# Splitting the load of the second K into three transfers

## The chip, the cores and the metric

The kernel runs on one core of a Trainium2 chip. The metric is device time in microseconds (us), the median of several runs. A core has a matrix engine (TensorE, PE in the profile, with its weight loads as PEld), a vector engine (VectorE, DVE), a scalar engine (ScalarE, ACT), GpSimd (POOL) and SyncE (SP), which here only issues transfers. Data are moved between the chip's main memory (HBM) and the on-chip memory (SBUF, 128 partitions) by sixteen DMA engines.

## The reference

It is the forward and backward pass of attention for one query row and 32 heads, with 8,192 keys and values of 128 numbers each, in bfloat16:

```python
scores = jnp.einsum('bhqd,bhkd->bhqk', q, k) * scale      # (1, 32, 1, 8192)
attn = softmax(scores, axis=-1)
out = jnp.einsum('bhqk,bhkd->bhqd', attn, v)
# and the gradients of out, for a given grad_out, to q, k and v
```

The outputs are `out`, dq, dk and dv. K and V are 64 MiB each and are read once; dk and dv are as large and are written once. dk is the outer product of ds (the gradient of the scores) and q, dv that of the attention weights p and grad_out.

## The kernel before

Heads are taken two at a time: sixteen pairs, `t` from 0 to 15. The K of a pair is one tile of 128 partitions by 128 rows by 128 numbers, 32 KiB a partition and 4 MiB in all; partition p holds 128 neighbouring rows, so that a whole load reads 32 KiB in one run for each partition (`rows_of`). The same holds for V. There are three buffers for K and two for V, used in turn (`Kt`, `Vt`).

For each pair K is turned by VectorE (`k_block`, L197) and multiplied with q on TensorE (L205), which gives the scores; softmax follows (`s_back` to `p_of`). V is turned by TensorE (`v_bank`, L269) and copied by ScalarE (L275), or turned by VectorE (`v_block`, L293), and multiplied with grad_out into dp (`v_scores`, `v_wide`). From p and dp comes ds. V and K are then contracted with p and ds (`contract`, L341) for out and dq. At last VectorE writes dv and dk over V and K in place (`outer`, L363), and from there they are stored (`store`, L373).

A buffer's round is therefore load, read, overwritten, stored, loaded again. In the loop over `t`, the load of K for `t + 2` (L540) waits for the store of dk of pair `t - 1` out of the same buffer, and the load of V for `t + 2` (L542) for the store of dv of pair `t`. Loads and stores of K and V are all issued by SP, in the program's order, on one queue: a transfer that waits holds up those behind it. The order of the work is written out by hand (`tc.manual_schedule`). Completion of transfers is told by eight semaphores used in turn; a ninth transfer is issued when the one eight places earlier has landed.

The change lies at the start, ahead of all this: q and grad_out, then V and K of pair 0 in four quarters each (8 KiB a partition), then K and V of pair 1 whole:

```python
    load_v(0, 4)
    load_k(0, 4)
    load_k(1)
    load_v(1)
```

The third K (`load_k(2)`, L410) is issued once pair 0 no longer uses that buffer as room for its turned V. K of pair 1 is first read by `k_block(1, 0)` inside the loop's first round, V of pair 1 by `v_part(1, 0)` near the end of that round.

Of the kernel before, what the change touches and what calls it, by code (L numbers as in the profile page):

```python
# [20 lines left out]
SL = 8  # L21
# [6 lines left out]
def kernel(  # L28
# [11 lines left out]
    nc = tc.nc  # L40
    P = 128
    _, H, S, D = k.shape
    HP = H // 2
    NT = 2 * S // P
# [27 lines left out]
    Kt = {t: k_in[t % K_BUFS] for t in range(HP)}  # L72
    Vt = {t: v_in[t % V_BUFS] for t in range(HP)}

    def rows_of(x, t, a, b):
        return x[0, 2 * t:2 * t + 2].rearrange("h s d -> (h s) d").rearrange("(p n) d -> p n d", p=P)[:, a:b, :]

    def load(x, X, t, parts):
        L = NT // parts
        for c in range(parts):  # L80
            nc.sync.dma_start(X[t][:, c * L:(c + 1) * L, :], rows_of(x, t, c * L, (c + 1) * L))

    def load_k(t, parts=1):
        load(k, Kt, t, parts)

    def load_v(t, parts=1):
        load(v, Vt, t, parts)
# [3 lines left out]
    nc.scalar.dma_start(rows[:, 1, :], grad_out.rearrange("b h s d -> (b h s) d"))  # L91
    load_v(0, 4)
    load_k(0, 4)
    load_k(1)
    load_v(1)

    ident = consts.tile([P, P], BF16)
# [477 lines left out]
```

## Time and profile before

| | |
|---|---|
| median of 3 runs | 635.55 us (635.55 to 635.78) |
| profiled execution | 635.36 us, its span 633.6 us |
| DMA queue q1 (all loads and stores of SP) | 268.47 MB, 99.2% of sixteen engines' time |
| VectorE busy | 558.9 us, 88% of the span |
| TensorE busy | 428.7 us, 68% |
| ScalarE busy | 158.0 us, 25% |
| a whole load of K or V, from issue to landing | 19.3 us, median |

The span runs from the first to the last instruction that the profiler recorded; some 1.8 us of the execution's time lie around it. The DMA share is the mean over the sixteen engines: 1.00 means that all of them moved data all the time, and 0.25 that four did. A transfer is spread over the engines, each of which sets a completion mark of its own when its part has landed; a wait for the transfer ends with the last mark. The trace has the time of each mark, but not the number of the engine that set it.

### The profile page before, as it was taken

How to read it: one execution, taken by the hardware profiler on the slowest of the kernel's cores; microseconds unless marked ns; L12 is line 12 of the kernel's file. 1: busy time of each engine (PE TensorE's matmuls, PEld its weight loads, DVE VectorE, ACT ScalarE, POOL GpSimd, SP SyncE). 2: the span in 40 equal slices, each digit the busy share in tenths (PEclk: the TensorE clock that was granted, in tenths of full speed). 3: DMA queues.
4: the chain of work that ended last, by engine and by line, in shares of the span. 5: the costliest groups of instructions: out<-in, count | busy, mean ns of one | idle time of the engine just before them, and what ended most of it. 6: DMA issues, size and time to landing. Idle time of an engine off the chain costs nothing.

```text
span 633.6 us, 7259 instructions
## 1 busy us (share of the span) xinstructions
PE 428.7 (68%) x2876; PEld 231.2 (36%) x2876; DVE 558.9 (88%) x662; ACT 158.0 (25%) x407; POOL 9.5 (1%) x27
## 2 busy tenths in 40 slices
PE   6767777766685765847766676765768658576860
PEld 5225335242341523315342332523425233152630
DVE  3788997999979899998998989899898899989793
ACT  6013416031230412204031130311303113040520
POOL 2000000000000000000000000000000000000000
PEclk9879888879789777798878798687986878887865
DMA  8999999999999999999999999999999999999997
GB/s 355 440 428 398 438 418 415 425 430 409 432 433 431 435 431 431 435 432 431 429 431 430 432 431 430 430 432 438 436 426 434 431 434 427 432 430 429 426 414 325
DMA packets 12177, 268.92 MB, mean 424 GB/s; under 512 B 1520, under 2 KB 1520, under 8 KB 1520
## 3 DMA queue, kind: packets, MB, share of 16 engines
q1 hardware_dynamic: 12096, 268.47, 99.2%
q8 instruction: 22, 0.36, 0.2%
q14 instruction: 11, 0.09, 0.0%
q10 hardware_dynamic: 48, 0.01, 0.0%
HBM read 134.23 MB, written 134.23 MB: 424 GB/s over the span
## 4 chain that ended last, share of the span: by engine, by line
DVE 38%; DMA 27%; PE 22%; issue 9%; ACT 2%; DVEq 0%; SPq 0%; ACTq 0%
DVE XK_sb L197 15%; DMA K<-in_k_dram 14%; DMA out_dram<-K 13%; DVE K L363 11%; PE T_ps L269 10%; DVE V L363 6%; PE dp_ps L303 5%; PE acc_p L341 3%; PE dp_ps L286 2%; ACT XV_sb L275 1%; DVE sT L212 1%; DVE dpT L312 1%; PE m_ps L220 1%; DMA V<-in_v_dram 1%; DVE ds_rep L331 1%
## 5 line engine op out<-in xcount | busy, mean ns | idle before, releaser
L205 PE MATMUL s_ps<-XK_sb,q_win 128*128 128x512 bf16 x512 | 148.6, 431 | 50.5 <-DVE XK_sb L197 48.3
L197 DVE STREAM_TRANSPOSE XK_sb<-K 128x1024 f32<-128x1024 f32 x128 | 152.2, 1221 | 3.5 <-DMA K<-in_k_dram 3.3
L363 DVE TENSOR_TENSOR V<-p_rep,qd 128x2048 bf16<-128x2048 bf16 x128 | 152.0, 1203 | 3.2 <-DMA K<-in_k_dram 2.0
L363 DVE TENSOR_TENSOR K<-ds_rep,qd 128x2048 bf16<-128x2048 bf16 x128 | 147.8, 1207 | 0.1
L269 PE MATMUL T_ps<-ident_f,V 128*128 128x128 f32 x640 | 108.1, 333 | 0.3 <-DMA V<-in_v_dram 0.2
L205 PEld LDWEIGHTS <-q_win 128*128 128x128 bf16 x512 | 53.4, 106 | 138.6 <-issue 102.7
L269 PEld LDWEIGHTS T_ps<-ident_f,V 128*128 128x128 f32 x640 | 97.5, 176 | 14.5 <-ACT XV_sb L275 1.6
L275 ACT COPY XV_sb<-T_ps 128x512 f32<-128x512 f32 x144 | 79.0, 586 | 78.7 <-PE T_ps L269 78.3
L293 DVE STREAM_TRANSPOSE XV_blk<-V 128x1024 f32<-128x1024 f32 x48 | 59.6, 1241 | 9.1 <-PE dp_ps L303 8.7
L341 PE MATMUL acc_ds<-K,win_ds 128*32 128x512 bf16 x512 | 47.8, 540 | 27.8 <-ACT win_ds L241 27.8
L220 PE MATMUL m_ps<-ident_f,top 128*128 128x128 f32 x16 | 6.2, 389 | 72.6 <-DVE top L219 72.6
L303 PE MATMUL dp_ps<-XV_blk,do_wide 128*128 128x512 bf16 x192 | 51.2, 399 | 0.0
L182 ACT COPY q_win<-q_blk 128x16 bf16<-128x16 bf16 x16 | 4.2, 260 | 156.7 <-PE s_ps L205 156.2
L341 PE MATMUL acc_p<-V,win_p 128*32 128x512 bf16 x512 | 32.1, 394 | 2.6 <-ACT win_p L241 2.4
L341 PEld LDWEIGHTS <-win_ds 128*32 128x32 bf16 x512 | 15.9, 122 | 48.1 <-ACT win_ds L241 27.2
L220 PEld LDWEIGHTS m_ps<-ident_f,top 128*128 128x128 f32 x16 | 2.6, 161 | 79.4 <-issue 71.4
L286 PE MATMUL dp_ps<-XV_sb,do_win 128*32 128x512 bf16 x288 | 24.3, 413 | 8.1 <-ACT XV_sb L275 8.1
L230 ACT ACTIVATE e<-sT,nbias 128x128 f32<-128x128 f32 x16 | 8.2, 515 | 80.8 <-DVE nbias L227 80.8
L303 PEld LDWEIGHTS <-do_wide 128*128 128x128 bf16 x192 | 17.3, 100 | 28.3 <-issue 14.3
L312 DVE STREAM_TRANSPOSE dpT<-dp_ps 128x512 f32<-128x512 f32 x16 | 11.5, 717 | 13.9 <-PE dp_ps L303 13.0
L341 PEld LDWEIGHTS <-win_p 128*32 128x32 bf16 x512 | 13.0, 99 | 16.3 <-issue 6.7
L321 PE MATMUL m_ps<-pd,same 128*128 128x1 f32 x32 | 6.1, 260 | 18.8 <-DVE m_ps L315 18.8
(68 smaller groups left out, 203.4 us busy)
## 6 DMA issues: line engine op xcount, KB each, us to landing
K<-in_k_dram SPq DMA_DIRECT2D x15, 4096.0 KB, 19.3
V<-in_v_dram SPq DMA_DIRECT2D x14, 4096.0 KB, 19.3
out_dram<-K SPq DMA_DIRECT2D x14, 4096.0 KB, 26.3
out_dram<-V SPq DMA_DIRECT2D x14, 4096.0 KB, 18.4
V<-in_v_dram SPq DMA_DIRECT2D x8, 1024.0 KB, 9.6
out_dram<-V SPq DMA_DIRECT2D x8, 1024.0 KB, 12.8
K<-in_k_dram SPq DMA_DIRECT2D x4, 1024.0 KB, 16.3
out_dram<-K SPq DMA_DIRECT2D x2, 2048.0 KB, 11.9
```

The source lines that it names most:

```text
L197: nc.vector.transpose(X[:], Kt[t][:, c * BN:(c + 1) * BN, :].rearrange("p n d -> p (n d)").bitcast(F32).rearrange("p (n w j) -> p n w j", ...
L205: nc.tensor.matmul(x["s"][:], lhsT=q_win[:, 2 * w + e2, SL - 1 - c:SL - 1 - c + P], rhs=cols[:, w, e2], start=(c == 0 and w == 0 and e2 == 0),
L220: nc.tensor.transpose(x["m"][:, 128:256], top[:].to_broadcast([P, P]), ident_f[:])
L230: nc.scalar.activation(e[:].rearrange("p (c n) -> p n c", c=NB), x["sT"][:, :, 0:NB], ACT.Exp, bias=nbias[:], scale=scale, accum_out=rs[:])
L269: nc.tensor.transpose(T_ps[:, j, :], words[:, at * P:(at + 1) * P], ident_f[:])
L275: nc.scalar.copy(x["XV", z][:, i * TB:(i + 1) * TB, :], x.pop(("T", m))[:])
L286: nc.tensor.matmul(x["dp"][b * QD:(b + 1) * QD, :], lhsT=do_win[:, b // 2, e2, at:at + QD], rhs=cols[:, e2, :, b * QD:(b + 1) * QD], start ...
L293: nc.vector.transpose(X[:], Vt[t][:].rearrange("p n d -> p (n d)").bitcast(F32).rearrange("p (m r w j) -> p m r w j", r=SL, w=NW, j=QD)[:, ...
L303: nc.tensor.matmul(st[t]["dp"][:], lhsT=do_wide[:, 2 * w + e2, at:at + P], rhs=cols[:, w, e2], start=False, stop=(r == SL // 2 - 1 and w = ...
L312: nc.vector.transpose(dpT[:].rearrange("p m r -> p (m r)"), x.pop("dp")[:])
L341: nc.tensor.matmul(acc[which][b * QD:(b + 1) * QD, :], lhsT=win[which][:, g, at:at + QD], rhs=X[:, 4 * g:4 * g + 4, :].rearrange("p n d -> ...
L363: nc.vector.tensor_tensor(X[:, a:b, :].rearrange("p n (a b) -> p n a b", b=R), x[which][:, a:b, :].unsqueeze(2).to_broadcast([P, BN, D // ...
```

## The change

The load of the second K (pair 1, 128 rows a partition) is made of three transfers. The first brings 120 of the 128 rows (called columns of the tile in the title) to all 128 partitions. The other two bring the last eight: one to partitions 0 to 123, one to partitions 124 to 127. All three are issued by SP, in this place and order. `P`, `NT` are 128 and `SL` is 8. Nothing else differs.

```diff
     load_v(0, 4)
     load_k(0, 4)
-    load_k(1)
+    nc.sync.dma_start(Kt[1][:, 0:NT - SL, :], rows_of(k, 1, 0, NT - SL))
+
+    for i, j in ((0, P - 4), (P - 4, P)):
+        nc.sync.dma_start(Kt[1][i:j, NT - SL:NT, :], rows_of(k, 1, NT - SL, NT)[i:j])
     load_v(1)
```

## The prediction

> **What bounds the kernel now.** I read the busy row of the DMA engines first, then the DMA queues, then stretches of the span, then the chain that ended last, and at the end the start of the SP queue.
>
> ```profile
> DMA  8999999999999999999999999999999999999997
> ...
> q1 hardware_dynamic: 12096, 268.47, 99.2%
> q8 instruction: 22, 0.36, 0.2%
> ...
> HBM read 134.23 MB, written 134.23 MB: 424 GB/s over the span
> ```
>
> All loads and stores run on one queue, q1, and its packets fill 99.2% of the time of all sixteen DMA engines. VectorE, the next busiest, has 88%. The stretches show the rate:
>
> ```profile
> 155.00:350.00 195.00, 132.93 (x865) 68.92 (x864) 181.74 (x209) 44.51 (x121) 1.56 (x5) 0.83 1.00 432
> 350.00:600.00 250.00, 174.29 (x1117) 92.86 (x1120) 226.78 (x263) 59.33 (x154) 1.87 (x6) 0.84 1.00 432
> ```
>
> The last two columns are the DMA share and GB/s: 1.00 and 432 for 445 us on end, so 27.0 GB/s for one engine. 268.47 MB at 432 GB/s are 621.5 us of a 633.6 us span. The kernel is bound by its DMA engines, and each carries its own sixteenth of every transfer. Hence what counts is not the mean engine but the last one. The end of the span shows how far they stand apart:
>
> ```profile
> 628.50:629.00 0.50, 0.00 (x0) 0.00 (x0) 0.00 (x0) 0.00 (x0) 0.00 (x0) 0.50 0.71 298
> ...
> 630.00:630.50 0.50, 0.00 (x0) 0.00 (x0) 0.00 (x0) 0.00 (x0) 0.00 (x0) 0.50 0.43 180
> ...
> 631.00:631.50 0.50, 0.00 (x0) 0.00 (x0) 0.00 (x0) 0.00 (x0) 0.00 (x0) 0.50 0.31 131
> 631.50:632.00 0.50, 0.00 (x0) 0.00 (x0) 0.00 (x0) 0.00 (x0) 0.00 (x0) 0.50 0.12 49
> ```
>
> A share of 0.31 is five engines, 0.12 is two: most engines are done while two still work. The trace also holds a completion mark of each engine for each transfer. For the last store the sixteen marks stand at 0 to 0.15 us after the first for six engines, and at 1.2, 1.6, 2.1, 2.2, 2.6, 3.1, 3.3, 3.4, 3.7 and 4.0 us for the other ten. At 18 us they lay within 0.41 us. The instruction fetches (q8) are one cause: one of 16 KB ran at 19.2 us, and at the next mark one engine was 1.29 us later than before while the fifteen others kept their places. An engine that has fallen behind stays behind, since none is idle for long.
>
> ```profile
> 332.03 27.35 DMA out_dram<-K
> 359.43 19.29 DMA K<-in_k_dram
> 378.74 1.25 DVE XK_sb L197
> ```
>
> The chain in the middle goes store of K, load of K into the same buffer, first transpose on it. The load is issued when the *last* engine has finished the store, and the transpose starts when the last engine has landed the load.
>
> **The change, part by part.** Sum and parts stand against the profiled execution: 635.36 us, a span of 633.6 and 1.8 around it; the median of the runs is 635.55, 0.19 above.
>
> *Bytes.* None is added: one 4 MiB load becomes 120 of 128 columns (30,720 B a partition), and the last eight (2,048 B a partition) go in two transfers, of 124 and of 4 partitions. The first spreads like every load here, eight partitions to an engine. Its engines have 8 x 2,048 = 16,384 B less: at 27.0 GB/s, 0.61 us less for each of the sixteen.
>
> *How 124 partitions spread.* Every transfer of the trace has 128 or 32 partitions and sixteen marks, eight or two whole rows an engine; none shows 124. At one end sixteen engines take seven or eight rows each, and nothing changes. At the other, one engine takes all: 253,952 B, 9.4 us, less the 0.61. Between them: the shares in the trace are all equal, and the largest number up to sixteen that divides 124 is four, with 31 rows each; 4 partitions also make four shares of one row. I take four engines, because equal shares are what every row of the trace has.
>
> [...]
>
> *Price on the four.* 31 + 1 rows of 2,048 B are 65,536 B in place of 16,384: 49,152 B more, 1.82 us at 27.0 GB/s. Small pieces cost a little more: the quarter loads at the start (8 KB pieces) land 2.48 us apart, a quarter of a full load's 9.67 to 9.70 is 2.42, so 0.06 over eight pieces, 7 ns a piece. The four have 40 pieces where they had 8: 32 x 7 ns = 0.23. Together +2.05 us on four engines, -0.61 on twelve. Upper end: the fetch of 16 KB cost its engine 1.29 us where 27.0 GB/s gives 0.61, about twice as much; if rows that cross into other engines' partitions fare like that, 49,152 B cost 3.9 us.
>
> *What of it reaches the end.* From 25 to 600 us the engines have no idle time in which four late ones could catch up (shares 0.99 to 1.01 in all stretches), so the 2.05 lasts to the end, on top of what each engine is late already. The end moves by 2.05 less the distance by which the latest of the four now lies before the latest of all. If the four hold the last or next-to-last engine (4.0 and 3.7 above), that is 2.05 or 1.8 us; with 3.4 as their latest 1.4; with 3.1 1.1. I take 1.8.
>
> *Issue and waits.* SP issues two more transfers, 0.34 us each. A queue entry is only issued when the transfer eight places before it has landed (they share a completion semaphore):
>
> ```profile
> 3.23 3.05 SPq L81 DMA_DIRECT2D K<-in_k_dram  x5
> 8.42 0.33 SPq L81 DMA_DIRECT2D V<-in_v_dram  x1
> 17.47 0.33 SPq L81 DMA_DIRECT2D K<-in_k_dram  x1
> 36.69 13.53 SPq L373 DMA_DIRECT2D out_dram<-V  x4
> ```
>
> The second V's load went out at 8.42, when V's second quarter had landed (8.40). Two places later it waits for the fourth quarter, landed at 13.39. The third K's load behind it, at 17.47, waits for TensorE (dp_ps) and stays. The engines have work until the first K's last quarter at 22.9 to 24.6 us and then the second K's, so this costs nothing; uncovered it would be 5 us. The stores at 36.69 wait for VectorE, not for these.
>
> *Landing of the second K.* Its last mark was at 34.31 and comes 2 us later, 36.4 at most by the price taken. The first transpose that reads it starts at 40.73: 4.3 us of cover. The second V lands at 44.03, and TensorE first reads it at 53.07: 9 us. The waits list puts one 2.0 us wait of VectorE, at 34.30, down to this load; if that is so and VectorE falls 2 us back, its four stores still come in time, for the engines are busy with the third K until 52.4 to 55.1.
>
> Sum: +1.8 us from the engines, 0 from issue, 0 from waits: 637.2 on the profiled execution, 637.3 on the median.
>
> **The rivals.** *The four are early engines.* The six engines at 0 to 0.15 us have 3.8 us to spare; with +2.05 against -0.61 for the ten that end the kernel, they would still finish 1.2 us before them. Then the end comes 0.6 us earlier: 634.9, not slower. It decides as soon as one of the four lies less than 2.66 us before the last engine. Against it: four engines drawn blindly from sixteen miss all ten late ones in 15 of 1,820 cases. For it: they need not be a blind draw, since fetches fall on some engines again and again and four neighbours may all be spared; the trace does not name engines.
>
> *The small transfers use all sixteen engines.* Then it doesn't do what it says, and the time stays: 635.5 to 635.7. Against it are the equal shares of all transfers here.
>
> *Crossing costs double, or one engine takes all.* +3.9 (639.4) or +8.8 (644). The doubled fetch speaks for the first, but that fetch competed with the engine's own row of data, and here the small rows are themselves the queue's next work.
>
> [...]
>
> **How the numbers follow.** Four engines with a late one among them: 0.60, of which 0.53 at +1.3 or more and 0.07 below that. Early engines 0.26, all sixteen 0.07, double or one engine 0.07. Under 0.2% (1.27 us) a difference can hardly be told from none on this kernel. Slower: 0.53 + 0.07 = 0.60. Within: 0.07 + 0.21 + 0.07 = 0.35. Faster by over 0.2%: 0.05, the part of the early-engine case in which later fetches also meet the twelve better. The likeliest case alone spans 636.7 to 637.7. The range starts at the early-engine time, 634.8, and reaches to 639.0, short of the doubled price; it leaves out about 0.1.
>
> **What would show it.** After the change the second K's marks should fall in two groups, four about 2.7 us later than the rest. The marks of the last store should span more than 4.0 us (up to 6.6), and the stretch from 630 to the end show four or fewer engines at work for longer. VectorE's and TensorE's busy times stay. The prediction is wrong if the four are the six's (the last store's marks then move together, span below 4), or if no group of four appears.

## The result and the profile after

| | before | after |
|---|---|---|
| median of 20 runs | 635.28 us (634.79 to 636.38) | 636.38 us (635.64 to 637.07) |
| profiled execution (span) | 635.36 (633.6) | 636.30 (634.5) |

The ratio is 1.0018, with a 95% interval of 1.0012 to 1.0024: the change makes the kernel 0.8 to 1.5 us slower, 1.1 by the medians. The prediction said 637.3 in a range of 634.8 to 639.0; its direction and range hold, and its +1.8 was too much by 0.7. The measured +0.18% falls just inside the band of 0.2% to which I gave 0.35, not into "slower by over 0.2%", to which I gave 0.60.

The page of the changed kernel, its lines on the DMA queues:

```profile
DMA  8999999999999999999999999999999999999997
...
q1 hardware_dynamic: 12232, 268.47, 99.0%
q8 instruction: 22, 0.36, 0.2%
...
HBM read 134.23 MB, written 134.23 MB: 423 GB/s over the span
```

The bytes are the same. There are 136 more packets, 128 of them rows of 2 KB and eight completion marks. Four stretches of the changed kernel (the last two columns are the DMA share and GB/s):

```profile
32.00:36.50 4.50, 2.63 (x26) 1.22 (x29) 2.12 (x4) 1.32 (x3) 0.00 (x0) 0.50 0.97 256
36.50:42.00 5.50, 3.02 (x34) 1.28 (x30) 5.40 (x10) 0.59 (x2) 0.31 (x1) 0.81 1.00 429
155.00:350.00 195.00, 131.27 (x860) 69.22 (x859) 178.36 (x206) 44.71 (x121) 1.56 (x5) 0.84 1.00 431
350.00:600.00 250.00, 171.38 (x1105) 91.31 (x1104) 227.47 (x264) 58.11 (x152) 1.87 (x6) 0.85 1.00 431
```

And the first of them in the kernel before:

```profile
32.00:36.50 4.50, 2.92 (x28) 1.24 (x32) 2.49 (x3) 1.32 (x3) 0.00 (x0) 0.64 1.08 466
```

This is the one place where something went wrong. From 32.0 to 36.5 us the engines are as busy as before (0.97) and move 256 GB/s in place of 466. (So short a stretch is coarse, since a packet is counted where it starts: 466 is above the 432 of the long stretches. The difference is far larger than that.) Busy and slow at once means that each packet takes longer: the trace has the 2 KB rows at 137 ns on average, and the 32 KB packets of the second V beside them at about 2.1 us on average (33 to 35 us) and 2.2 at most, where one usually takes 1.22. From 36.5 us on the rate is back.

The issue queue of the changed kernel does what was forecast:

```profile
6.04 0.33 SPq L94 DMA_DIRECT2D K<-in_k_dram  x1
8.56 4.13 SPq L97 DMA_DIRECT2D K<-in_k_dram  x2
13.52 0.36 SPq L81 DMA_DIRECT2D V<-in_v_dram  x1
17.76 0.35 SPq L81 DMA_DIRECT2D K<-in_k_dram  x1
```

The second V goes out at 13.52 in place of 8.42, the third K 0.3 us later than before; neither leaves an engine without work. The end of the changed kernel:

```profile
630.00:630.50 0.50, 0.00 (x0) 0.00 (x0) 0.00 (x0) 0.00 (x0) 0.00 (x0) 0.50 0.16 66
631.00:631.50 0.50, 0.00 (x0) 0.00 (x0) 0.00 (x0) 0.00 (x0) 0.00 (x0) 0.50 0.15 66
631.50:632.00 0.50, 0.00 (x0) 0.00 (x0) 0.00 (x0) 0.00 (x0) 0.00 (x0) 0.50 0.12 49
632.50:633.00 0.50, 0.00 (x0) 0.00 (x0) 0.00 (x0) 0.00 (x0) 0.00 (x0) 0.50 0.08 33
```

From 630 us only two or three engines work, and in the last us one (0.08 of sixteen). Before, seven still worked at 630.0 to 630.5 (0.43). The kernel now waits for fewer and later engines.

**The marks.** The completion marks of the engines, read from the trace, tell the rest. The two small transfers have four marks each (the first at 36.33 to 37.18 us), so both ran on four engines. (Each has one more mark at the time of its issue, 9.00 and 12.86 us, long before its rows move; it tells of no engine.) At the second V the sixteen marks are: eleven within 0.44 us, one at 2.1, by its times the engine that an instruction fetch had hit at 19.3 us, and 2.8, 2.9, 3.0 and 4.3, which by their times follow the four marks of the small transfers. The whole study rests on four numbers a kernel: first and last mark of the second V, where the split has just been paid, and of the last store, which is the end.

| kernel, profiled execution | second V: first, last | last store: first, last |
|---|---|---|
| before | 42.32, 44.03 | 628.70, 632.68 |
| before, second profile (`c_copy`) | 42.34, 44.05 | 626.37, 632.24 |
| after | 43.50, 47.76 | 629.84, 633.58 |
| after, second profile (`c_after`) | 43.59, 47.53 | 629.66, 633.37 |
| 8 columns, 128 partitions (`e_even8`) | 42.49, 44.25 | 628.00, 632.16 |
| 8 columns, 64 + 64 (`e_half8`) | 42.96, 44.94 | 628.39, 634.43 |
| 16 columns, 64 + 64 (`e_half16`) | 43.83, 46.66 | 626.79, 633.35 |
| 32 columns, 64 + 64 (`e_half32`) | 45.09, 48.18 | 628.92, 635.52 |
| 32 columns, 124 + 4 (`e_four32`) | 51.55, 65.65 | 646.60, 651.77 |
| 8 columns, 127 + 1 (`e_one8`) | 47.49, 54.79 | 634.49, 639.65 |
| extra work aside (`e_aside`) | 42.43, 46.99 | 629.15, 633.19 |
| change at the last K (`e_late8`) | 42.31, 43.91 | 627.37, 636.04 |

The last mark of one profile differs from that of the next profile of the same kernel by 0.2 to 0.4 us at the end, the first mark by up to 2.3, so verdicts on time go by the ratios of repeated runs, and the marks by their early values, which repeat within 0.3 us.

### The profile page after: what moved, and what is told of

It is laid out like the page before. It is cut to its first block, busy times and chain, and to the rows that moved or that the text cites. A ratio compares the mean times of both kernels' runs of the same rounds, so it can differ in the third digit from the quotient of the medians.

```text
span 634.5 us, 7262 instructions
## 1 busy us (share of the span) xinstructions
PE 427.4 (67%) x2876; PEld 229.8 (36%) x2876; DVE 559.4 (88%) x662; ACT 157.5 (25%) x407; POOL 9.3 (1%) x27
## 4 chain that ended last, share of the span: by engine, by line
DMA 37%; DVE 32%; PE 19%; issue 7%; ACT 3%; DVEq 0%; POOL 0%; SPq 0%; ACTq 0%; POOLq 0%
DMA out_dram<-K 21%; DMA K<-in_k_dram 15%; DVE XK_sb L200 13%; DVE K L366 10%; PE T_ps L272 9%; DVE V L366 5%; PE dp_ps L306 3%; PE dp_ps L289 2%; ACT XV_sb L278 2%; PE acc_p L344 2%; PE s_ps L208 2%; DVE sT L215 1%; PE m_ps L223 1%; DVE dpT L315 1%; DVE mx L220 1%
## 5 line engine op out<-in xcount | busy, mean ns | idle before, releaser
L272 PE MATMUL T_ps<-ident_f,V 128*128 128x128 f32 x640 | 104.7, 327 | 0.0
L272 PEld LDWEIGHTS T_ps<-ident_f,V 128*128 128x128 f32 x640 | 95.4, 173 | 14.2 <-issue 2.6
L344 PE MATMUL acc_ds<-K,win_ds 128*32 128x512 bf16 x512 | 49.1, 551 | 27.8 <-ACT win_ds L244 27.8
## 6 DMA issues: line engine op xcount, KB each, us to landing
V<-in_v_dram SPq DMA_DIRECT2D x14, 4096.0 KB, 19.3
K<-in_k_dram SPq DMA_DIRECT2D x14, 4096.0 KB, 19.3
```

Of the source, the lines that this page charges most:

```text
L272: nc.tensor.transpose(T_ps[:, j, :], words[:, at * P:(at + 1) * P], ident_f[:])
L344: nc.tensor.matmul(acc[which][b * QD:(b + 1) * QD, :], lhsT=win[which][:, g, at:at + QD], rhs=X[:, 4 * g:4 * g + 4, :].rearrange("p n d -> ...
```

## The experiments

After the result there were two readings of the +1.1. One is that of the prediction: four engines have more to do, and the last of them ends the kernel. The other is the pause just seen: the small rows slow all engines, and the twelve, which should have come 0.6 us earlier, come 1.2 later (42.32 to 43.50).

**Does chance hide in the profile of before?** The kernel before, unchanged.

> The kernel before, unchanged, for a second profile. In the profiled execution of before, nearly all sixteen engines stall together for 0.5 to 1.5 us at about 50, 90, 109 and 150 us, and the changed kernel's profile has none of it. If these stalls belong to the kernel, they stand at the same places again and the first marks at 161 to 165 us come within 0.3 us of before's. If they are chance, they stand elsewhere or are missing, and the marks at 160 us come 1 to 2 us earlier; then the last store's marks show how far the end moves by chance alone (some 0.5 us).

634.92 us; the last mark 0.44 us earlier than in the first profile, the marks at 160 to 164 us 1.5 to 1.7 earlier. Stalls stand at 40 to 60 and 100 to 120 us and are fewer: part of them is chance. This second profile is the cleaner one to compare with.

**Do small rows cost anything by themselves?**

```diff
-    load_k(1)
+    nc.sync.dma_start(Kt[1][:, 0:NT - 8, :], rows_of(k, 1, 0, NT - 8))
+    nc.sync.dma_start(Kt[1][:, NT - 8:NT, :], rows_of(k, 1, NT - 8, NT))
     load_v(1)
```

> The second K in two transfers: 120 columns and the last eight, both over all 128 partitions, so that every engine keeps its share. Queue theory (the end moves because four engines get more bytes): within 0.1% of before; the marks of the second K and V stay together as before, 32 more 2 KB rows cost nothing, eight cost 0.06 us. Pause theory (small rows of a split load slow all engines for some 1.7 us): +1 us or more, 1.0015 or above, and 32 KB packets of about 2 us behind the small rows.

1.0001 (0.9993 to 1.0010). The 2 KB rows take 84 ns each, and the second V's marks move by 0.15 us. Eight columns split off as small rows cost nothing that these runs can tell, with each piece over all 128 partitions.

**Four times the dose on four engines.**

```diff
-    load_k(1)
+    nc.sync.dma_start(Kt[1][:, 0:NT - 32, :], rows_of(k, 1, 0, NT - 32))
+    for i, j in ((0, P - 4), (P - 4, P)):
+        nc.sync.dma_start(Kt[1][i:j, NT - 32:NT, :], rows_of(k, 1, NT - 32, NT)[i:j])
     load_v(1)
```

> As the change, but with the last 32 columns on the four engines in place of eight: 196,608 B more on four engines (7.3 us at 27.0 GB/s), 65,536 B less on the other twelve (2.4 us). Queue theory: the four lie 9.7 us behind the twelve at the second V and stay there to the end, so the end moves by 7.3 us less at most 1.3, about 1.010 to 1.012. Pause theory (all engines are slowed while the small rows run, and the four's lag is caught up later): at most four times the measured 1.1 us, 4.4 us or 1.007, with the last store's marks no further apart than before (4 us).

1.0279 (1.0263 to 1.0294), 17.7 us: both theories fall short by far. Two stretches of this kernel show why:

```profile
30.00:52.00 22.00, 12.66 (x88) 5.20 (x89) 18.04 (x26) 2.79 (x8) 0.31 (x1) 0.76 1.01 194
72.00:82.00 10.00, 9.16 (x102) 6.29 (x95) 8.30 (x11) 7.54 (x17) 0.31 (x1) 1.00 0.52 197
```

For 22 us, while the four engines bring their 8 KB rows, all engines together move 194 GB/s with a share of 1.01. The twelve others, which have less to do, are 9.2 us late at the second V for it. Then the four marks stand 12 to 14 us behind the first one, and this is more than the queue of issued transfers covers: from 72 to 82 us half the engines' time is idle (0.52). The cause is in the issue queue of the same kernel:

```profile
37.49 13.53 SPq L375 DMA_DIRECT2D out_dram<-V  x4
77.88 7.59 SPq L81 DMA_DIRECT2D V<-in_v_dram  x4
```

The loads of the third V wait until the last engine has stored the first quarter, at 77.8; before, they went out at 57.68. So a large lag is caught up, by making the others wait.

**One engine alone.**

```diff
-    load_k(1)
+    nc.sync.dma_start(Kt[1][:, 0:NT - 8, :], rows_of(k, 1, 0, NT - 8))
+    for i, j in ((0, P - 1), (P - 1, P)):
+        nc.sync.dma_start(Kt[1][i:j, NT - 8:NT, :], rows_of(k, 1, NT - 8, NT)[i:j])
     load_v(1)
```

> The last eight columns over 127 partitions and 1, so that, if shares are equal, one engine takes them all: 262,144 B where it had 16,384, 9.1 us more at 27.0 GB/s, and 9.3 with its 128 small rows. Queue theory: one mark 9.7 us behind the fifteen others from the second V to the last store, the end 8 to 9.3 us later, 1.0125 to 1.0147. Pause theory: one engine crosses into others one row at a time, so the pause is short, and the end moves by less than 2 us. If the rows go to sixteen engines after all: no change.

1.0115 (1.0102 to 1.0129), 7.3 us: the order of size of the queue theory, and well above the 2 us of the other. 127 partitions do run on one engine: the transfer has one mark, at 45.16. But one mark 9.7 us behind fifteen undisturbed ones is not what the second V shows; it shows fifteen that are 5 us late and one that is 10.7 late. The issue queue and a stretch of this kernel tell the fifteen's part:

```profile
8.50 25.52 SPq L96 DMA_DIRECT2D K<-in_k_dram  x2
34.06 0.36 SPq L81 DMA_DIRECT2D V<-in_v_dram  x1
```

```profile
33.00:35.00 2.00, 0.54 (x8) 0.32 (x12) 0.20 (x1) 1.22 (x3) 0.00 (x0) 0.50 0.07 26
```

SP was held in these two issues until 34.0 us; only then did the second V go out, and from 33 to 35 us nearly nothing moved (26 GB/s, about one engine). That the one engine had come to the rows about then is an estimate: 127 rows of 84 ns, the time of one in `e_even8`, back from its mark at 45.16 us are 34.5 us. With 31 rows an engine, as in the change, the same issue took 1.66 us in place of 23.04, and the second V behind it did not go out later for it.

**Where does the pause come from: from few engines, or from foreign partitions?** In a transfer of 64 partitions all sixteen engines take part (it has sixteen marks), with four rows each if the shares are equal, so each engine brings rows to both halves. The trace doesn't show which partitions an engine fills, in these transfers or in a whole load; that they are others here is the assumption of the crossing theory (below).

```diff
-    load_k(1)
+    nc.sync.dma_start(Kt[1][:, 0:NT - 8, :], rows_of(k, 1, 0, NT - 8))
+    for i, j in ((0, HF), (HF, P)):
+        nc.sync.dma_start(Kt[1][i:j, NT - 8:NT, :], rows_of(k, 1, NT - 8, NT)[i:j])
     load_v(1)
```

The same with 16 and with 32 in place of 8 (`e_half16`, below, and `e_half32`).

> [...] Crossing theory (a row that lands in partitions which another engine is filling slows both; that gave the pause of the change, in which 32 KB packets took 2.06 us for 1.21): all marks of the second V 0.6 to 1.9 us later, spread as before, the end later by the same, 1.001 to 1.003. Four-engine theory (the pause comes of the crowding on few engines): no pause, within 0.1% of before.

> The same with 32 columns, four times the bytes and no engine with more than its share. Crossing theory: the marks of the second V 2.4 to 7.6 us later with the spread of before, the end likewise, 1.004 to 1.012. Four-engine theory: no change, so that the 17.7 us of the run with 32 columns on four engines come of the four alone.

1.0014 (1.0005 to 1.0023) and 1.0042 (1.0028 to 1.0056). The first mark of the second V comes 0.62 and 2.75 us later, with no group of four behind the rest (spread 2.0 and 3.1 us, for 1.7). The stretch from 32 us, first with eight columns over all partitions, then with 32 in two halves:

```profile
32.00:36.50 4.50, 2.51 (x26) 1.23 (x30) 1.86 (x4) 1.39 (x5) 0.00 (x0) 0.54 1.16 493
```

```profile
32.00:36.50 4.50, 2.63 (x26) 1.32 (x30) 2.03 (x4) 1.32 (x3) 0.00 (x0) 0.50 1.15 320
```

The share is the same, the rate is not. It isn't the number of engines: with equal shares on all sixteen there is a pause as soon as a transfer covers half of the partitions instead of all. Whether the rows then meet partitions that another engine is filling, or half of the partitions take in fewer rows at a time whoever brings them, these runs don't tell apart. The size of the pause fits twice the time for the bytes: eight columns are 16,384 B an engine, 0.61 us at 27.0 GB/s, and the mark is 0.62 late; for 16 columns it is 1.2 and 1.5 is measured, for 32 columns 2.4 and 2.75.

**Which of the two decides in the change, the four's lag or the pause?** Each was made alone, in about the size that the change has. For the lag, a transfer that the kernel doesn't need was put behind a whole load, from HBM to HBM; it adds bytes that the kernel before doesn't move:

```diff
     load_k(1)
+    aside = nc.dram_tensor("aside", (4, 2, 192 * D), BF16).ap()
+    nc.sync.dma_start(aside, k[0, 2:6, 0:384, :].rearrange("h (c n) d -> h c (n d)", c=2))
     load_v(1)
```

> The second K in one load as before, and behind it a transfer that the kernel doesn't need: four rows of 98,304 B from HBM to HBM, which, if shares are equal, runs on the same four engines and touches no partition of the on-chip memory. At 27.0 GB/s it makes the four 3.6 us late at the second V, as late as the change made them (3.5 to 3.7), and does nothing to the other twelve. Last-engine theory with the four deciding: the end moves by as much as with the change, 1.0012 to 1.0024. If what the change costs is the pause of the twelve (1.2 us at the second V) and the four's lag is covered by engines that fall behind later: no change, within 0.05%.

> The last 16 columns over two halves of the partitions, all sixteen engines alike, crossing rows twice as large as with eight columns. With eight columns the first mark of the second V came 0.62 us later and the end about 0.9, with 32 columns 2.75 and 2.7; so here 1.2 to 1.5 at the second V and at the end, 1.002. If a pause on all engines of the size that the twelve had in the change (1.2) moves the end by 1.1 to 1.3, the pause alone is enough to account for the change; if it moves it by less than 0.6, the four are needed.

Lag alone: 1.0021 (1.0012 to 1.0030). The twelve are undisturbed (first mark 42.43), four marks stand 3.7, 3.8, 3.8 and 4.6 us behind them (whether of the same four engines as in the change, the marks don't tell). Pause alone: 1.0025 (1.0016 to 1.0035), with a first mark 1.5 us late (1.2 in the change) and the last one 2.6 (3.7 in the change). The change, which has both, costs 1.0018. So either alone gives a cost of this size, and the two don't add up. That fits an end that is a maximum over engines and not a sum; how much of the change's own 1.1 us belongs to each stays open, since this pause is larger than the change's.

**Is the four's lag worn off with time?** The change's split, at the last K instead of the second:

```diff
-        if 0 < t and t + 2 < HP:
+        if 0 < t and t + 2 < HP - 1:
             load_k(t + 2)
+        elif t + 2 == HP - 1:
+            nc.sync.dma_start(Kt[t + 2][:, 0:NT - SL, :], rows_of(k, t + 2, 0, NT - SL))
+            for i, j in ((0, P - 4), (P - 4, P)):
+                nc.sync.dma_start(Kt[t + 2][i:j, NT - SL:NT, :], rows_of(k, t + 2, NT - SL, NT)[i:j])
```

> The change's split at the last K's load (pair 15, landing at 574 us) in place of the second. Last-engine theory (the end is that of the engine that is last; four are 3.8 us later, twelve 1.2): what the fetches and chance do to the engines between 35 and 555 us then lies before it, and the end moves by 1.2 us if none of the four is among the late ones, by up to 3.8 if one of them is last already: 1.002 to 1.006. If the lag of the four needed hundreds of us to be caught up, the late split costs the full 3.8. If the split only costs where it met the start of the kernel: no change.

1.0058 (1.0045 to 1.0070): 3.7 us, three times the price of the early split, and as much as the last of the four lost at the second V (44.03 to 47.76). The stretch of the late split, and the same stretch of the kernel before in its second profile:

```profile
565.00:578.00 13.00, 8.92 (x86) 3.48 (x79) 10.72 (x15) 1.65 (x6) 0.31 (x1) 0.87 1.02 365
```

```profile
565.00:578.00 13.00, 9.97 (x92) 3.83 (x85) 11.90 (x16) 1.94 (x7) 0.31 (x1) 0.87 1.03 440
```

And the end of the late split's span, then that of the kernel before in its second profile:

```profile
630.00:633.00 3.00, 0.00 (x0) 0.00 (x0) 0.00 (x0) 0.00 (x0) 0.00 (x0) 0.50 0.33 137
633.00:635.50 2.50, 0.00 (x0) 0.00 (x0) 0.00 (x0) 0.00 (x0) 0.00 (x0) 0.50 0.06 27
```

```profile
630.00:633.00 3.00, 0.00 (x0) 0.00 (x0) 0.00 (x0) 0.00 (x0) 0.00 (x0) 0.50 0.08 33
```

After 633 us a single engine (0.06 of sixteen) keeps the kernel open. Its mark in the V load right behind the split already stands 3.2 us behind the next one. It was among the last before the split, as near as the marks tell: three of the four marks of the 124 rows stand at 569.6 to 571.5 us, the fourth at 577.8, and 31 rows of 0.11 us take that one back to about 574.4, where the 120 columns have their last mark (574.15). So here, by this estimate, little or nothing lay between the latest of the four and the end.

**Does the same engine stay last?** The changed kernel, unchanged.

> The changed kernel again, for a second profile. Last-engine theory: once more the engine that is last at the second V, one of the four, is last at the end, and the end is 1 to 2 us after that of the second profile of before (632.24 us for the last mark). If which engine is last changes from one execution to the next, one of the twelve ends it, and the first marks move by 1.2 us with it.

636.09 us; last mark 1.13 us after that of `c_copy`. In both profiles of the change the last mark stays by itself from the second V to the end: at least 0.6 us, in the second one 0.3, behind the next in every transfer, so it is one engine throughout, and by its start one of the four. In the profiles of before the last two marks come within 0.04 us of each other on the way, and the lead can pass from engine to engine.

## Why the prediction was right, and where it was off

*What bounds the kernel: right.* In every run the time followed the last engine's mark: the twelve profiled executions ended 2.6 to 2.8 us after it. With bytes and engine work unchanged, splits moved the end by 0 to 17.7 us.

*How 124 partitions spread: right.* Four marks for 124 partitions, four for 4, one for 127: equal shares, as the rows of before had it. That both small transfers run on the same four, which the sum took (31 + 1 rows an engine), no run shows, since a mark names no engine. The four marks of the second stand 0.19 to 0.25 us behind those of the first, one behind each, which would fit it.

*Bytes: right where nothing interferes.* The 120 columns landed 0.57 us earlier (first mark 32.61 to 32.04), forecast 0.61.

*Price on the four: the term that was mis-sized.* I took +2.05 us and kept 3.9 as the upper end, dismissed because "here the small rows are themselves the queue's next work". Measured at the second V, the last mark of the four is 3.5 to 3.7 us later than the last of before: the upper end. The three of the four that nothing else delayed stand at 46.27 to 46.46 us, where all engines of before but two stood at 42.32 to 42.80: 3.5 to 4.1 later. (The fourth took 10.4 us for its share of the second V in place of 9.7; a packet of 1.88 us beside an instruction fetch at 42.7 us would account for it.) The rival "crossing costs double", to which I gave 0.07 together with "one engine takes all", had the right price, though not the time at the end.

*The twelve: wrong in sign.* -0.61 became +1.2. The prediction had the doubled price fall on the crossing rows alone; the packets beside them suffer as much (1.22 to about 2.1 us). With this the rival of the early engines lost its ground, twelve engines that come earlier, whichever engines the four were.

*What of it reaches the end: wrong the other way.* I took a slack of 0.25 us, from the assumption that the four hold the next-to-last engine. The slack was about 2.5: of 3.5 to 3.7 us at the second V 0.7 to 1.3 remain at the last store, by the two profiles compared, and 1.1 by the medians. The marks and packets show two parts of it. First, the kernel before loses time on all engines together that the change doesn't lose. The stretch from 37 to 55 us, before and after:

```profile
37.00:55.00 18.00, 11.95 (x73) 5.43 (x74) 17.90 (x21) 1.55 (x4) 0.31 (x1) 0.91 1.00 411
```

```profile
37.00:55.00 18.00, 12.14 (x70) 4.58 (x63) 17.90 (x22) 0.96 (x3) 0.31 (x1) 0.79 1.00 428
```

The 32 KB packets that start from 49 to 52 us take 1.55 us on average before, 1.60 in its second profile, and 1.22 after; the stalls at 90, 109 and 150 us follow. So the mean of the sixteen marks of a transfer, 1.9 us later in the change at the second V, is only 0.8 later at 540 us than in the second profile of before, and 0.7 earlier than in the first. Second, engines fall behind one by one: the spread of before grows from 1.7 us at 44 us to 6.2 at 593 in the second profile, so an engine that is late early need not be the last one at the end. This part is what is left, 0.4 to 1.2 us. My reading of the final marks alone missed both. The late split shows the other side: it has the stalls at 50 and 109 us behind it, meets an engine that is last already, and costs the full 3.7. Why the change lacks the stalls stays open, so the size of the slack is measured and only in part explained.

*Persistence: right up to a point.* The last engine of the change is never caught up by the next one. Instruction fetches put it further back again and again: at 143, 238, 346 and 453 us, each time beside a fetch, the distance of its mark from the next grows by 0.8 to 0.9 us (from 0.62 to 1.54 at the first). A lag of 12 us (`e_four32`) runs into the waits of the issue queue, where the other engines stand idle for it. I had named the depth of the queue as a cover for late landings only.

*Issue and waits: right.* V's load at 13.52, forecast 13.39; no idle engine. The 2.0 us wait of VectorE at 34 us is not the load's:

```profile
DVE V L366 <- PE acc_p L344: 2.0, 1, 2.0
```

In the changed kernel, whose K lands later, the list names TensorE's contraction for the same wait of the same length.

*The sign of being wrong: it came, and misled.* The prediction named marks of the last store that span less than 4 us as the sign that the four are early engines and that it is wrong. They span 3.7 in both profiles of the change, yet a group of four did appear and one of them ends the kernel. The two profiles of before have 4.0 and 5.9, so this span was no test.

The two errors, up to +1.7 on the four and 2.3 too little slack, are each larger than the whole effect and partly cancel to the 0.7 by which the forecast was high. That one engine decides, and that it is one of the four, was foreseen; that the time came out so near is in part luck.

## What to carry to other kernels

Where all DMA engines are busy all the time (a share of 1.00 here), look at the last engine and not at the mean: the marks of each transfer, or the DMA share in the last few us, show how far they stand apart. Split a load by columns, so that each piece still spans all 128 partitions (1.0001 here); a split by partitions cost all engines a pause here, about the time of the split bytes once more, even where the shares were equal. A delay of one engine cost here what went beyond the engine that would have been last at the end without it: the same split cost 1.1 us early and 3.7 late. Don't count on the early discount, since part of it came of stalls that failed to appear and are not explained.

## What the runs showed of the hardware

- In the change, rows of a transfer over part of the partitions and the packets of whole loads beside them were both slow: 2 KB rows took 137 ns in place of 84, 32 KB packets about 2.1 us in place of 1.22, and the core's rate was 256 GB/s for 4.5 us in place of 432. A transfer from HBM to HBM on four engines (`e_aside`) left the other twelve where they were (first mark at 42.43 us, before 42.32; 466 GB/s in the same 4.5 us, as before). That the rows meet partitions which other engines are filling would fit both; it is not shown. With 32 columns on four engines the rate was 194 GB/s for 22 us, at a busy share of 1.01: the busy share doesn't show it, the rate does.
- Issuing a transfer was itself held: with 127 rows waiting on one engine SP stood in the next issue until 34.0 us, 23 us after it began; with 31 rows on each of four it was 1.7 us.
- Stalls of 0.5 to 1.5 us that hit nearly all engines at once occur in some profiles (at 50, 90, 109 and 150 us in the first of before, fewer in the second) and hardly in the two of the change after 37 us (none in the first, a trace at 109 us in the second). In those that lack them from 72 to 500 us the marks lay at least 2.6 us apart at 90 us, in those that have them at most 2.5. That engines which run close together disturb each other is a guess from these spreads, and an early lag would then pay for itself in part; no run tests it, and it stays open.
